# Half-array transposes beside the score matmuls, merged normalisation and tanh, in a fused attention and gated-convolution kernel

## The chip, the cores and the metric

The kernel runs on one core of one Trainium2 chip. The metric is the device time of one execution, in microseconds (us). A kernel was timed in three or more runs, beside runs of the kernel before on the same chip. "Fast" and "slow" are the states given to each run; with one core, slow means over 1.5% above the fastest run of the same kernel. The profile calls the engines PE (TensorE), DVE (VectorE), ACT (ScalarE), POOL (GpSimd) and SP (SyncE).

## The reference

q, k and v have shape (8, 8, 576, 64): 8 batches, 8 heads, 576 positions, 64 features.

```python
scores = scale * np.matmul(q, k.transpose(0, 1, 3, 2))
scores = np.where(block_i >= block_j, scores, -1e9)     # causal by blocks of 64
attn = softmax(scores);  x = attn @ v                   # heads side by side: (8, 576, 512)
gate_pre = sum(conv_w[k] * xp[:, k:k + S, :] for k in range(5))   # causal, per channel
return (sigmoid(gate_pre) * (x @ w_val)) @ w_out
```

## The kernel before

The work is cut into 32 pairs of heads, four to a batch. Each turn of the main loop computes the scores and exponentials of pair p, the weighted sum and normalisation of pair p-1, the query/key transposes of pair p+1, and a share of the convolution, of the value projection ("val") and of the output projection ("out") of an older batch. A "conv pair" (every second one) has a convolution. I call the loop up to pair 31 the loop, and what follows the start of pair 31 the drain. The last 64 positions of each batch, the "tails", are loaded, cast and transposed once per batch.

Every transpose uses the whole array: 8 for queries and keys, 5 for the attention output, 4 per batch for the tails. PE writes its results into four single-bank tiles G0 to G3 and two double-bank score tiles S.

```python
GT = [psG.tile([128, 512], fp32, tag=f"G{i}", name=f"G{i}") for i in range(4)]

def trans(p, bank=None):                       # cut: the special case of pair 0
    for i in range(2):
        for c in range(4):
            o = 512 * i + 128 * c
            nc.tensor.transpose(out=rr[i][:, o:o + 128], in_=t[0:128, c, 2 * i:2 * i + 2, 0:64],
                                identity=ident16[0:128, 0:128])
    # one DVE copy of 128x1024
    nc.vector.tensor_copy(out=o[0:128].rearrange("p i (s n) -> p i s n", n=4), in_=src[0])

def avs(p, banks):                             # weighted sum, then normalisation, head by head
    for h in range(2):
        av(p, h, banks[h])
        norm(p, h, banks[h])

# main loop, from pair 5 on (cut)
        s_tile(p, 0)
        s_tile(p, 1)
        avs(p - 1, (0, 1) if cv else (1, 0))
        if p < NP - 1:
            trans(p + 1, 2)
        if not early:
            out(3)
        ...
        s_tile(p, 2)
        mask(p)
        ...
        if cv:
            conv(gs // 2, (0, 1), early)
        xtrans(p - 1, 2 if cv else 0)
        # val, val
        if p in T_TRANS:                       # LAST thing in the turn
            trans_tails(T_TRANS[p], 2 if cv else 0 if early else 1)

# drain (cut): one output tile and one val alternate, over a ring of four banks
    for h in range(NP - LAG - 1, NP):
        for x in (0, 1):
            if len(outs) > 1:
                out()
            val(h // 2, 2 * (h % 2) + x)
```

Two tables decide where the tails of a batch are cast by POOL and where PE transposes them. From the fourth batch on, both are pair 4b-4: the same turn of the loop.

The softmax here doesn't subtract the row's maximum and nothing guards it: scores larger than these inputs give would overflow.

## Time and profile before

Median 199.47 us of the first three runs (198.42 to 202.71). The profiled run has a span of 196.9 us. I split it at the starts of the first score matmuls of pairs 0, 5, 13 and 31.

| stage | us | what limits it |
|---|---|---|
| head: pairs 0 to 4 | 19.65 | loads and first casts, then PE with holes |
| pairs 5 to 12 | 44.72 | PE, with holes |
| pairs 13 to 30 | 93.29 | PE, no holes: busy 93.30 of 93.30 us |
| drain | 32.08 | PE almost alone, no scores left |

From the page of the kernel before come three lines (those between are left out). They give each engine's busy time, the TensorE clock granted in 40 slices (tenths), and one group of instructions (busy time, mean ns of one, idle before it).

```profile
PE 181.9 (92%) x3701; PEld 124.3 (63%) x3701; DVE 131.8 (67%) x287; ACT 139.2 (71%) x193; POOL 81.1 (41%) x166
PEclk9999997999999999999999999999999999999999
L167 DVE COPY qkT<-G 128x1024 f16<-128x1024 f16 x31 | 37.7, 1217 | 3.7 <-PE G L156 3.5
```

The PE timeline of pair 19 before, a conv pair (start, duration, engine, line, operation, output<-input, count). A group's cost is read from start to start.

```profile
102.61 0.74 PE L33 MATMUL S<-qkT 64*128 64x512 f16 x6
103.28 0.60 PE L33 MATMUL G<-v,pt 128*128 128x65 f16 x14
...
104.20 0.61 PE L156 MATMUL G<-ident,qk 128*128 128x128 f16 x8
104.65 1.03 PE L33 MATMUL G<-w_out,gv 128*128 128x512 f16 x4
...
106.92 0.45 PE L252 MATMUL G<-ident,x 128*128 128x128 f16 x5
107.20 1.14 PE L33 MATMUL G<-xt,w_val 128*128 128x288 f16 x8
108.28 0.61 PE L33 MATMUL S<-qkT 64*128 64x512 f16 x6
```

Eight query/key transposes take 104.65 - 104.20 = 0.45 us and five output transposes 0.28: 56 ns each, 0.73 us together. The output projection follows the transposes without a gap.

### The profile page before, as it was taken

What the parts mean: (1) busy time and instruction counts of PE and PEld (TensorE: products, weight loads), DVE (VectorE), ACT (ScalarE), POOL (GpSimd) and SP (SyncE); (2) the same over time, 40 slices, a digit from 0 to 9 for tenths busy, and PEclk for the clock granted to TensorE, in tenths of its full rate; (3) what the DMA queues carried; (4) which work ended last, traced back from release to release, by engine and by line L of the source; (5) the groups of instructions that cost most, each with busy time, mean ns of one, the idle gap of its engine ahead of it and who ended that gap; (6) DMA issues with size and microseconds to landing.
All of it is one profiled execution on the core that took longest, in us unless ns stands there. A gap on an engine that the chain in (4) does not pass through costs nothing.

```text
span 196.9 us, 8701 instructions
## 1 busy us (share of the span) xinstructions
PE 181.9 (92%) x3701; PEld 124.3 (63%) x3701; DVE 131.8 (67%) x287; ACT 139.2 (71%) x193; POOL 81.1 (41%) x166
## 2 busy tenths in 40 slices
PE   3997859989799799999999999999999999999992
PEld 0475737666666477667667777677767675756550
DVE  5377756998668486768776767678676868542451
ACT  0778784777788788877888778887888797545321
POOL 7276742573564644345434543464445422100000
PEclk9999997999999999999999999999999999999999
DMA  5999999999999557976887687878665111143355
GB/s 159 258 285 258 264 326 314 218 261 220 268 226 289 154 170 195 271 223 178 228 249 224 190 243 215 235 215 238 203 201 145 57 57 57 58 158 149 133 208 213
DMA packets 70337, 40.43 MB, mean 205 GB/s; under 512 B 48149, under 2 KB 64789, under 8 KB 70298
## 3 DMA queue, kind: packets, MB, share of 16 engines
q1 hardware_dynamic: 68288, 39.07, 72.0%
q10 hardware_dynamic: 2010, 0.80, 1.8%
q8 instruction: 29, 0.48, 1.0%
q14 instruction: 10, 0.08, 0.2%
HBM read 30.42 MB, written 9.44 MB: 202 GB/s over the span
## 4 chain that ended last, share of the span: by engine, by line
PE 76%; DMA 9%; DVE 5%; SPq 3%; issue 2%; ACT 1%; ACTq 1%; POOL 1%; POOLq 0%; DVEq 0%
PE G L33 47%; PE S L33 17%; PE G L156 6%; PE G L252 5%; DMA tlst<-in_k_dram 3%; DMA qks<-in_k_dram 3%; DMA vs<-in_v_dram 3%; DVE w_val L388 2%; SPq L107 1%; DVE qkT L167 1%; DVE x L238 1%; SPq L86 1%; PE G L142 1%; DVE gv L292 1%; ACT pt L190 1%
## 5 line engine op out<-in xcount | busy, mean ns | idle before, releaser
L190 ACT ACTIVATE pt<-S 128x1024 f16<-128x1024 f32 x96 | 94.7, 1025 | 21.9 <-PE S L33 19.5
L206 POOL MEMSET pt<- 64x384 f16 x32 | 13.2, 412 | 76.5 <-ACT pt L190 76.3
L167 DVE COPY qkT<-G 128x1024 f16<-128x1024 f16 x31 | 37.7, 1217 | 3.7 <-PE G L156 3.5
L33 PE MATMUL G<-xt,w_val 128*128 128x288 f16 x256 | 38.7, 286 | 1.3 <-issue 1.3
L292 DVE SCALAR_TENSOR_TENSOR gv<-th,G 128x288 f16<-128x288 f32 x64 | 28.3, 453 | 14.0 <-PE G L33 12.3
L33 PEld LDWEIGHTS <-pt 128*128 128x128 f16 x960 | 32.1, 99 | 7.5 <-issue 3.5
L130 POOL CAST qk<-qks 128x1024 f16<-128x1024 f32 x31 | 32.4, 1047 | 10.1 <-DMA qks<-in_k_dram 8.1
L33 PE MATMUL G<-w_out,gv 128*128 128x512 f16 x144 | 36.5, 379 | 0.0
L33 PE MATMUL G<-v,pt 128*128 128x65 f16 x896 | 34.7, 195 | 1.6 <-POOL pt L206 1.1
L314 ACT COPY osb<-G 128x512 f32<-128x512 f32 x31 | 18.2, 587 | 22.2 <-PE G L33 19.5
L238 DVE TENSOR_TENSOR x<-G,rc 128x320 f16<-128x320 f32 x64 | 31.5, 492 | 2.2
L33 PE MATMUL S<-qkT 64*128 64x512 f16 (+1 forms) x248 | 29.1, 302 | 3.6 <-ACT pt L190 2.2
L33 PEld LDWEIGHTS <-qkT 64*128 64x128 f16 x496 | 16.1, 95 | 24.3 <-issue 20.0
L33 PEld LDWEIGHTS <-w_val 128*128 128x128 f16 x256 | 23.9, 98 | 8.9 <-issue 1.5
L237 DVE RECIPROCAL rc<-G 128x5 f32<-128x5 f32 x64 | 12.1, 189 | 20.1 <-PE G L33 20.0
L254 DVE COPY xt<-G 128x576 f16<-128x576 f16 x32 | 14.6, 456 | 13.3 <-PE G L252 13.0
L156 PE MATMUL G<-ident,qk 128*128 128x128 f16 x256 | 20.5, 225 | 2.2 <-DVE qk L127 1.8
L135 POOL CAST v<-vs 128x512 f16<-128x512 f32 x32 | 20.2, 632 | 0.5
L33 PEld LDWEIGHTS <-gv 128*128 128x128 f16 x144 | 12.9, 98 | 9.9
L156 PEld LDWEIGHTS <-qk 128*128 128x128 f16 x256 | 15.4, 101 | 4.2 <-DVE qk L127 2.7
L33 PE MATMUL G<-xt,DG 32*32 32x288 f16 x640 | 16.9, 288 | 0.3 <-DVE x L238 0.3
L33 PE MATMUL S<-xt,DG 32*32 32x288 f16 x640 | 16.8, 287 | 0.0
(58 smaller groups left out, 148.5 us busy)
## 6 DMA issues: line engine op xcount, KB each, us to landing
out_dram<-osb SPq DMA_DIRECT2D x35, 256.0 KB, 2.3
qks<-in_q_dram SPq DMA_DIRECT2D x32, 256.0 KB, 4.3
qks<-in_k_dram SPq DMA_DIRECT2D x31, 256.0 KB, 4.6
vs<-in_v_dram SPq DMA_DIRECT2D x62, 128.0 KB, 4.8
tlst<-in_q_dram SPq DMA_DIRECT2D x8, 128.0 KB, 4.6
vtst<-in_v_dram SPq DMA_DIRECT2D x8, 128.0 KB, 4.5
w_st<-in_moe_w_val_dram SPq DMA_DIRECT2D x2, 512.0 KB, 6.7
w_st<-in_moe_w_out_dram SPq DMA_DIRECT2D x2, 512.0 KB, 6.9
```

Source lines behind the costliest of these rows:

```text
L33: nc.tensor.matmul(out=out, lhsT=lhsT, rhs=rhs, start=start, stop=stop, skip_group_check=True)
L130: nc.gpsimd.tensor_copy(out=o, in_=s)
L135: nc.gpsimd.tensor_copy(out=v16s[p % NV][0:128, 0:4, 0:2, 0:64], in_=s)
L156: nc.tensor.transpose(out=rr[i][:, o:o + 128], in_=t[0:128, c, 2 * i:2 * i + 2, 0:64], identity=ident16[0:128, 0:128])
L167: nc.vector.tensor_copy(out=o[0:128].rearrange("p i (s n) -> p i s n", n=4), in_=src[0])
L190: nc.scalar.activation(out=pts[p % NPT][0:128, 0:2, 512 * t:512 * t + 512], in_=s[0:128, 0:2, 0:512], func=AF.Exp, bias=0.0, scale=0.125)
L206: nc.gpsimd.memset(pt[64:128, 0:2, 0:1536].rearrange("p h (t s) -> p h t s", t=3)[:, :, :, 0:64], 0.0)
L237: nc.vector.reciprocal(out=rc[0:128], in_=O[:, :, 64:65])
L238: nc.vector.tensor_tensor(out=x16[p][0:128, 0:5, h, 0:64], in0=O[:, :, 0:64], in1=rc[0:128].to_broadcast([128, 5, 64]), op=ALU.mult)
L254: nc.vector.tensor_copy(out=xts[b % NX][0:128, g, 4:4 + SEQ], in_=r[:, 0:SEQ])
L292: nc.vector.scalar_tensor_tensor(out=gv[u][0:128, x, bi, hf, 0:288], in0=t[0:128, x, 0:288], scalar=1.0, in1=r[0:128, 0:288], op0=ALU.add, ...
L314: nc.scalar.copy(out=o[0:128], in_=r[0:128, 0:512])
```

## The change

The intent is to halve the PE time of the transposes. Each is split in two 64-row halves that work in different row halves of the array and write to different banks, two at once. They move next to the score matmuls, which use the array in 64-row halves too. G0 and G1 become one two-bank tile G, so that one normalisation and one tanh cover both heads or both groups of channels. G2 and G3 (called GS) take all transposes.

```diff
-    GT = [psG.tile([128, 512], fp32, tag=f"G{i}", name=f"G{i}") for i in range(4)]
+    G = psG.tile([128, 2, 512], fp32, tag="G", name="G")
+    GS = [psG.tile([128, 512], fp32, tag=f"G{i}", name=f"G{i}") for i in (2, 3)]
+    def transpose(o, x, r):
+        hs = slice(64 * r, 64 * r + 64)
+        nc.tensor.transpose(out=o, in_=x, identity=ident16[hs, hs])
+    def trans_mm(p):                     # 16 half transposes; xt_mm: 9
+                for r in range(2):
+                    o = 256 * i + 64 * c
+                    transpose(half(r)[:, o:o + 64], t[64 * r:64 * r + 64, c, 2 * i:2 * i + 2, 0:64], r)
+    def norm(p):                         # both heads in one instruction
+        nc.vector.tensor_tensor(out=x[0:128].rearrange("p i h d -> p h i d"), in0=O[:, :, :, 0:64],
+            in1=rc[0:128].to_broadcast([128, 2, 5, 64]), op=ALU.mult)
     # main loop (cut)
         s_tile(p, 0)
         s_tile(p, 1)
-        avs(p - 1, (0, 1) if cv else (1, 0))
-        trans(p + 1, 2)
+        half_mm(p)              # q/k of p+1, output of p-2, and the TAILS if their pair has come
+        trans_ev(p + 1, 0)      # DVE copies, one per bank
+        xt_ev(p - 2, 0)
+        avs(p - 1)
+        norm(p - 1)
+        if cv:
+            out(2)
+            score()             # third score tile, mask
+            conv(gs // 2)
+            vals(h, (2, 3))
+        else:
+            score(); out(2)     # cut: `out` first in the pairs of T_LAST
+            vals(h, (0, 1))
-        if p in T_TRANS:
-            trans_tails(T_TRANS[p], ...)
     # drain (cut): two vals on the two banks of G, output tiles on G2 and G3
+        for i in range(2):
+            if len(outs) > 1:
+                out(2 + i)
+            if i == 0:
+                vals(h, (0, 1))
```

In the new order, pair 4b-4 transposes the tails in two rounds over two pairs.

## The prediction

> **What bounds it now.** The page gives TensorE (PE) 92% of the span and 76% of the chain that ended last. From 67 us to the end each 10 us window shows PE 9.9 to 10.0 busy, while VectorE (DVE) has about 7.3, ScalarE (ACT) 8, DMA 0.77. The timeline there repeats every 10.4 us per two head pairs (5.2 per pair) with practically no PE wait (PE on ACT: 2.2 us in the whole run). Between 27 and 67 us the PE does have holes (1.1 us for a POOL memset, 1.0 for ACT, about 2 for DVE behind the weight scaling); before 27 us the waits are DMA. The last 30 us (no scores left) are PE-dense again.
>
> **What the change removes.** In the timeline 8 query/key transposes take 0.45 us start to start, 5 output transposes 0.28: 56 ns each. Score matmuls 64x64 in the same kernel run as row-half pairs: 8 in 0.11 us, 28 ns a pair. If the half transposes pair likewise (16 and 9 instructions = 8 + 5 slots), they cost 0.22 + 0.14 us: 0.37 us less PE per pair, plus 0.11 per batch of tails. Switches: [...] the trace shows about 0.1 us more at each change (scores to full-array). But the old order has 9 changes per two pairs and so has the new: transposes only change sides. I count no gain there.
>
> **What it adds and moves, on DVE.** A 1024-element copy of 1217 ns becomes two of 512 (691 as measured for the first pair): +165 ns. The xt copy (456) becomes about 323 + 290: +157. Tails 420 become four of about 220. Normalisation (2 x (189+492)) becomes about 195 + 825: -340. Every second gate pair is merged: -150 per two pairs. Sum: about zero; DVE stays at 3.6 to 4 us a pair. Two tanh of 422 become one of 672: ACT little changed (about 4.1 us a pair start to start). Neither becomes the bound at 4.8 us a pair.
>
> **Critical path.** All PE savings are on it from 67 to 166 us (19 pairs, ideal 7 us). But fewer, shared banks give new waits: the merged normalisation is ready only after both halves, one copy chain frees the two transpose banks. Laying the durations end to end I find about 0.2 us of PE wait before the output projection in a conv pair, 0.2 where the half transposes wait for the previous gate, 0.5 per batch when tails copies go first. So I expect about 4.9 to 5.05 us a pair: 3 to 5 us saved. In 27 to 67 us: fewer bank conflicts with ACT, but the transposes now stand before the weighted sum and wait for the POOL cast: net -1 to -3 us. Tail: same work, two output banks instead of four, merged gates: +0 to +1.
>
> **Prediction.** 193.8 us, range 189.5 to 197.5. Faster by over 2%: 0.68; within 2%: 0.28; slower: 0.04.
>
> **What would show it.** Half transposes starting in pairs every 28 ns (right), or 16 taking 0.45 us again (wrong). Two-pair period of 9.7 to 10.1 us. PE waits on DVE (qkT/xt copies, normalisation, gate) appearing, some tenths of a us per pair; PE busy below 10 of 10. DVE busy total within 5 us of 132; ACT within 2 us of 139. Span before the first output projection shorter by 1 to 3 us.
>
> **What would make it wrong.** Half transposes that do not overlap (gain gone, about 199); DVE chain longer than laid out, so that conv and vals wait every pair (197+); or the new order hiding those waits fully and removing the holes before 67 us (189).

## More of the kernel before

The windows of the kernel before, one per stage. Columns are given in the header: window and its length, busy time and count of each engine, granted clock, DMA share and GB/s.

```profile
core 0: us, PE busy (x) PEld busy (x) DVE busy (x) ACT busy (x) POOL busy (x), PEclk, DMA share, GB/s
7.18:26.83 19.65, 16.17 (x295) 11.70 (x295) 13.61 (x29) 15.24 (x17) 12.24 (x21) 1.00 1.20 269
26.83:71.55 44.72, 39.86 (x901) 28.47 (x901) 32.63 (x70) 33.84 (x46) 22.18 (x39) 0.96 0.93 239
71.55:164.85 93.30, 93.30 (x2045) 65.58 (x2044) 68.20 (x148) 74.48 (x104) 41.47 (x79) 1.00 0.69 196
164.85:196.90 32.05, 28.39 (x451) 16.98 (x450) 13.18 (x31) 13.71 (x25) 1.64 (x5) 0.99 0.40 147
```

PE has no gap in the third stage and the full clock in it. DVE (68 of 93 us) and ACT (74 of 93) have slack.

## The result, and the profile after

A ratio below is the mean time of one kernel's fast runs over that of the other's in the same rounds, so it is not quite the ratio of the medians quoted with it. The kernel after took 218.05 us (median of four, 215.96 to 220.18), the kernel before beside it 198.94: ratio 1.095, 95% interval 1.082 to 1.108. It is slower by nearly a tenth. The output is correct.

The profiled run, at 220.18 us, is slow. Its mean granted clock (0.960) is like that of the three fast runs (0.958 to 0.967). I read waits and their places from it; the 2 to 4 us by which its span exceeds theirs are not placed. The three fast runs average 217.35 us. The profiles of e3, e8 and e14 are of runs labelled slow too.

| stage | before | after | difference |
|---|---|---|---|
| pairs 0 to 4 | 19.65 | 28.02 | +8.4 |
| pairs 5 to 12 | 44.72 | 45.15 | +0.4 |
| pairs 13 to 30 | 93.29 | 100.24 | +6.9 |
| drain | 32.08 | 37.97 | +5.9 |

The page of the kernel after, the lines that answer to those above (those between are left out). Its chain of work that ended last breaks off after 4% of the span, so stages and waits must serve instead.

```profile
PE 188.5 (86%) x4117; PEld 123.8 (57%) x4117; DVE 127.0 (58%) x295; ACT 138.8 (64%) x175; POOL 81.0 (37%) x166
PEclk9999959985999999999999799999999999999999
L165 DVE COPY qkT<-G 128x512 f16<-128x512 f16 x63 | 42.6, 683 | 15.1 <-PE G L140 15.1
```

The windows of the kernel after, the same stages and columns:

```profile
6.99:35.00 28.01, 23.07 (x354) 16.35 (x354) 14.46 (x35) 15.24 (x17) 13.20 (x22) 0.88 1.17 280
35.00:80.15 45.15, 37.75 (x996) 26.36 (x996) 30.83 (x76) 32.34 (x38) 21.47 (x40) 0.92 0.81 198
80.15:180.39 100.24, 92.95 (x2282) 62.23 (x2276) 64.73 (x149) 75.02 (x95) 41.63 (x79) 0.98 0.62 172
180.39:218.40 38.01, 30.78 (x472) 17.67 (x471) 12.98 (x24) 14.21 (x23) 1.05 (x3) 0.99 0.36 133
```

In the third stage PE is busy 92.95 of 100.24 us. It had no idle time there before and has 7.3 us now, about as much as the stage has grown. No other engine has become the limit: DVE and ACT are busy as long as before, in a longer stage. The PE waits for something, now and then.

The PE timeline of pair 19 after (the conv pair shown before):

```profile
113.08 0.89 PE L33 MATMUL S<-qkT 64*128 64x512 f16 x6
113.79 0.41 PE L140 MATMUL G<-ident,qk 64*128 64x64 f16 x16
114.02 0.31 PE L140 MATMUL G<-ident,x 64*128 64x64 f16 x9
114.26 0.60 PE L33 MATMUL G<-v,pt 128*128 128x65 f16 x14
...
115.15 0.20 PE L33 MATMUL G<-v16t,pt 128*128 128x65 f16 x1
115.41 1.02 PE L33 MATMUL G<-w_out,gv 128*128 128x512 f16 x4
...
117.67 1.15 PE L33 MATMUL G<-xt,w_val 128*128 128x288 f16 x8
118.76 0.61 PE L33 MATMUL S<-qkT 64*128 64x512 f16 x6
```

The half transposes pair as hoped: 16 in 0.23 us, or 28 ns for two. But the pair takes 5.68 us against 5.67. The output projection starts 0.26 us after the last weighted-sum matmul, where one slot is 0.03: it waits for its bank.

PE, then POOL, in pair 20 after, the first pair of a batch's tails. In brackets: idle before, and the releaser.

```profile
119.20 0.56 PE L140 MATMUL G<-ident,qk 64*128 64x64 f16 x16
119.59 0.31 PE L140 MATMUL G<-ident,x 64*128 64x64 f16 x9
121.48 0.23 PE L140 MATMUL G<-ident,tl 64*128 64x64 f16 x4 [1.59 <-POOL tl L116]
121.65 0.60 PE L33 MATMUL G<-v,pt 128*128 128x65 f16 x14
```

```profile
118.72 1.04 POOL L130 CAST qk<-qks 128x1024 f16<-128x1024 f32 x1
119.69 0.62 POOL L135 CAST v<-vs 128x512 f16<-128x512 f32 x1
120.25 0.62 POOL L119 CAST v16t<-vtst 128x512 f16<-128x512 f32 x1
120.81 0.62 POOL L116 CAST tl<-tlst 128x512 f16<-128x512 f32 x1
```

The tails' cast is the fourth in POOL's queue of this very pair and ends at 121.43; PE stands still for 1.59 us until then. In the kernel before the same cast had the whole pair to finish in. The list of PE's waits after has as its first line:

```profile
PE G L140 <- POOL tl L116: 6.6, 5, 1.6
```

That is 6.6 us in five waits. Something more follows. Pair 20 takes 7.75 us, against 4.77 for an ordinary pair without convolution, and the wait accounts for only 1.6 of the 3.0. The granted clock is at half from 122.4 to 125.8 us. It is also at half from 26.8 to 33.6 and 47.3 to 54.1 us, and, by the durations of its matmuls (under "The clock" below), before 23.4 us.

### The profile page after: what moved, and what is told of

It reads as the page before. It is cut to its first block, busy times and chain, and to the rows that moved or that the text cites. A ratio compares the mean times of both kernels' runs of the same rounds, so it can differ in the third digit from the quotient of the medians.

```text
span 218.4 us, 9500 instructions
## 1 busy us (share of the span) xinstructions
PE 188.5 (86%) x4117; PEld 123.8 (57%) x4117; DVE 127.0 (58%) x295; ACT 138.8 (64%) x175; POOL 81.0 (37%) x166
## 5 line engine op out<-in xcount | busy, mean ns | idle before, releaser
L203 ACT ACTIVATE pt<-S 128x1024 f16<-128x1024 f32 x96 | 94.6, 1024 | 32.4 <-PE S L33 30.2
L165 DVE COPY qkT<-G 128x512 f16<-128x512 f16 x63 | 42.6, 683 | 15.1 <-PE G L140 15.1
L293 DVE SCALAR_TENSOR_TENSOR gv<-th,G 128x288 f16<-128x288 f32 (+1 forms) x49 | 26.0, 544 | 35.7 <-PE G L33 34.1
L33 PE MATMUL G<-v,pt 128*128 128x65 f16 x896 | 37.5, 202 | 0.5 <-ACT w_out L401 0.3
L33 PE MATMUL S<-qkT 64*128 64x384 f16 (+3 forms) x256 | 33.1, 324 | 4.2 <-ACT pt L203 2.7
L33 PEld LDWEIGHTS <-pt 128*128 128x128 f16 x960 | 34.8, 103 | 2.2
L250 DVE TENSOR_TENSOR x<-G,rc 128x640 f16<-128x640 f32 x32 | 26.4, 824 | 1.1
L140 PE MATMUL G<-ident,qk 64*128 64x64 f16 x512 | 16.0, 197 | 3.8 <-POOL qk L130 2.0
L178 DVE COPY xt<-G 128x320 f16<-128x320 f16 x64 | 17.1, 297 | 1.6 <-PE G L140 1.6
L140 PEld LDWEIGHTS <-qk 64*128 64x128 f16 x512 | 12.1, 100 | 9.1 <-POOL qk L130 2.9
L33 PEld LDWEIGHTS <-DG 32*32 32x32 f16 x1280 | 12.7, 88 | 7.9 <-issue 5.6
```

The costliest lines, as they stand in the source:

```text
L33: nc.tensor.matmul(out=out, lhsT=lhsT, rhs=rhs, start=start, stop=stop, skip_group_check=True)
L140: nc.tensor.transpose(out=o, in_=x, identity=ident16[hs, hs])
L165: (cp or nc.vector.tensor_copy)(out=qkT[p][0:128, 0:2, 256 * r:256 * r + 256].rearrange("p i (s n) -> p i s n", n=4), in_=half(r)[:, 0:512 ...
L178: nc.vector.tensor_copy(out=xts[b % NX][0:128, g, 4:644].rearrange("p (i r s) -> p i r s", r=2, s=64)[:, 0:n, r], in_=half(r)[:, 512:512 + ...
L203: nc.scalar.activation(out=pts[p % NPT][0:128, 0:2, 512 * t:512 * t + 512], in_=s[0:128, 0:2, 0:512], func=AF.Exp, bias=0.0, scale=0.125)
L250: nc.vector.tensor_tensor(out=x[0:128].rearrange("p i h d -> p h i d"), in0=O[:, :, :, 0:64], in1=rc[0:128].to_broadcast([128, 2, 5, 64]), ...
```

## The experiments

**The theories.** (A) The halves do what they should; the new order lost more than they save, by waits that PE did not have before, and these waits also cost clock. (B) The halves themselves harm: half-array work is too slow, or makes PE lose the full clock. (C) The merged instructions harm, by making PE wait for the later half. Fourteen kernels ran, all with correct results (no label e6 was used); the befores of the jobs were 198.3 to 199.97 us. Medians are compared with the kernel after (218.05) or with the kernel that was edited; where slow runs shift a median, the mean of the fast runs is given beside it.

### e1_cast: cast the tails one pair earlier

```diff
-    T_LOAD = {{1: 0, 2: 4, 3: 7}.get(b, 4 * b - 6): b for b in range(1, B)}
-    T_CAST = {{1: 3, 2: 7, 3: 9}.get(b, 4 * b - 4): b for b in range(1, B)}
+    T_LOAD = {{1: 0, 2: 4, 3: 7}.get(b, 4 * b - 7): b for b in range(1, B)}
+    T_CAST = {{1: 3, 2: 6, 3: 9}.get(b, 4 * b - 5): b for b in range(1, B)}
```

> The tail tiles (last 64 rows of q and k of a batch) are loaded and cast one head pair earlier, nothing else. Theory A (the POOL cast that the half transposes now wait for at the start of a pair costs 1.3 to 1.8 us of PE at pairs 16, 20, 24 and about 1.1 at pair 7, and the long idle also drops the TensorE clock at 47 and 122 us): the PE wait on POOL tl disappears, pairs 16, 20, 24 last 4.9 to 5.1 us instead of 6.0 to 7.8, the half-clock stretch at 122 us goes, and the kernel is 5 to 8 us faster than the changed one (210 to 213). Rival (half transposes are slow or the new chain of copies holds every pair): the wait moves to another engine and the time stays within 2 us of 218.

Measured: 209.15 us, ratio 1.054 (1.044 to 1.064). Pair 20 in e1:

```profile
114.03 0.31 PE L140 MATMUL G<-ident,x 64*128 64x64 f16 x9
114.16 0.24 PE L140 MATMUL G<-ident,tl 64*128 64x64 f16 x4
```

The hole is gone, and the three tails pairs 16, 20 and 24 take 4.53 us each instead of 6.29, 7.75 and 6.03. An edit of two tables is worth 8.9 us (7.9 by the fast runs alone: 209.43 against 217.35), more than its waits: with them went the half-clock stretches near 122 us and from 47 to 54 us. So the order of the queue on POOL was one of the two largest losses, beside the head. The stage of pairs 13 to 30 is still 95.07 us against 93.29 before, so the saving on the transposes is not yet seen.

### e2_warm: eight warm-up matmuls instead of four

The kernel issues dummy matmuls at its start. Their number is doubled.

```diff
-    warm(4)
+    warm(8)
     cast_qk(0, first=True)
```

> Eight dummy matmuls instead of four before the first transposes, so that the PE has no 2 us hole while the first loads arrive. Theory A (the head lost 8 us because the clock reached full speed at 23 to 34 us instead of 8 us[...]): full clock from about 5 to 8 us, pair 5 starts near 28 us instead of 35, total 5 to 8 us less (210 to 213). Rival ([...] the head order itself is slow): pair 5 still starts after 33 us and the total stays within 2 us of 218.

Measured: pairs 0 to 4 in 21.61 us, not 28.02, as expected. The total, 217.24 us (214.32 to 221.96; the two fast runs average 215.36), did not follow: 210 to 213 was expected. The clock row of e2's page:

```profile
PEclk9999699959999999969999799969999999999998
```

The kernel now reaches the full clock in the head, but loses it again near the tails' waits, at 93.3, 117.2 and 141.1 us. In the kernel after only one of these waits, at 122.4 us, did so in pairs 13 to 30. The head and the tails' waits are tied by the clock: with the tails' waits still there (7.1 us in six, 6.6 in five in the kernel after), a mend of the head raised the falls behind them in pairs 13 to 30 from one to three.

### e3_drain: output tiles and vals over four banks again, as before

In the drain, single vals and a ring of four banks, while the two-bank tile G stays.

```diff
+        ring = (0, 1, 2, 3) if h % 2 and h < NP - 1 else (2, 3, 0, 1)
+        for x in (0, 1):
+            if len(outs) > 1:
+                out(ring[2 * x])
+            val1(h // 2, 2 * (h % 2) + x, ring[2 * x + 1])
```

> The old drain in the changed kernel: after the last scores, values are gated one at a time and outputs and values go round all four banks. Theory A (two output banks and the merged gate and tanh make the PE wait 5 to 6 us in the drain): from the start of pair 31 to the end 33 to 34 us instead of 38, total 4 to 5 us less (213 to 214). Rival (the drain is longer for another reason, for example one more output tile and slower copies): under 1.5 us less.

A miss: the drain grew from 37.97 to 41.14 us, the total was 222.05 (fast runs: 220.3). The drain of e3 shows why:

```profile
189.13 1.02 PE L33 MATMUL G<-w_out,gv 128*128 128x512 f16 x4
190.87 0.65 PE L33 MATMUL G<-xt,w_val 128*128 128x288 f16 x4 [0.72 <-ACT osb L328]
```

The val writes one bank of G, and waits for ACT's copy of an output tile out of the other bank of G. A two-bank tile is one unit of dependence here; whether the chip or the framework makes it one is not shown. My edit had mixed two things, four banks and a tile that is only one unit; it says nothing against four independent banks.

### e4_all: e1, e2 and e3 together

The edit is the three diffs above, with no other line changed.

> The three edits together. If the three losses are separate and are all of the slowdown: about 199 to 202 us, the same as the kernel before within 2%, with regular pairs still at 10.4 to 10.5 us for two, so the saved PE time is still lost in them. If the losses overlap or something else is in play: above 205. If the regular pairs get faster once the stalls are gone: below 197.

A miss: 211.09 us, not 199 to 202. The drain took 41.14 us again (e3's fault), and pairs 0 to 4 took 25.65: the same head as e2's got the full clock at 4.3 us and lost it from 7.8 to 18.0. Pairs 13 to 30 took 93.00 us with every four pairs in 20.73, so even without holes the pairs only equal the before's 20.82. The 0.37 us per pair were still hidden by something in the ordinary pairs.

### e5_score_first: third score tile ahead of the output projection (on e1)

```diff
         if cv:
+            score()
             if not early:
                 out(2)
-            score()
             conv(gs // 2)
         ...
+            score()
+            out(2)
             vals(h, (0, 1))
```

> As e1_cast, and the last score tile of a pair is issued before the output projection in all late pairs, so the projection meets its bank after the transposes' copies are done. Theory A (in regular pairs the saved 0.37 us is given back by the projection waiting 0.16 to 0.23 us for the copies out of the transposes' bank, and by the exp that then comes late for the next pair's scores): conv pairs 5.4 us instead of 5.68, pairs with the last scores 4.6 instead of 4.77, about 0.7 us per four pairs, 2 to 4 us in all against e1_cast (205 to 207). Rival (ScalarE or VectorE holds the period, whatever the order on the PE): pairs keep 5.68 and 4.77, time within 1 us of e1_cast.

Measured: 203.76 us (ratio 1.023, 1.013 to 1.034, so unclear whether over 2% slower than before) against 209.15 for e1; 205 to 207 was expected, so a little better than that. Part of the 5.4 us is another phase of the clock in the head (24.56 against 27.34), and part is two single holes in e1's pairs 23 and 27 (0.8 and 1.7 us) that e5 does not have. In the loop, four pairs take 20.10 instead of 20.72. Start to start, PE spends in the conv pair 19:

| us | before | after | e5 |
|---|---|---|---|
| two score tiles | 0.67 | 0.71 | 0.44 |
| query/key and output transposes | 0.73 | 0.47 | 0.47 |
| weighted sums, to the next group | 0.92 | 1.15 | 1.03 |
| third score tile, output projection, convolution | 2.27 | 2.26 | 2.28 |
| two vals | 1.08 | 1.09 | 1.08 |
| sum | 5.67 | 5.68 | 5.30 |

(The numbers of before and after can be checked on the two timelines above; the before's 0.73 is 0.45 + 0.28. A "mode" below is the division of the array: matmuls on 64 rows or on all 128.) The transposes save 0.26 in the kernel after. They are paid back by 0.23 at the end of the weighted sums, where the output projection waits for its bank until DVE has copied the transposes out of it, and by 0.04 at the score tiles. The latter should have become 0.1 shorter, as in pair 18 (0.54 us before, 0.44 after), since no change of mode follows them any more; instead they wait 0.27 us against e5. In both kernels ACT copies the output tile before it does the exponential of the third score tile (in pair 18 the copy starts at 100.90 and the exponential at 101.38 us before, 111.52 and 112.00 after), and so frees the score tiles late. The same place in e5, where the score tile now stands before the output projection:

```profile
106.07 0.20 PE L33 MATMUL G<-v16t,pt 128*128 128x65 f16 x1
106.20 0.28 PE L33 MATMUL S<-qkT 64*128 64x256 f16 x2
106.53 1.04 PE L33 MATMUL G<-w_out,gv 128*128 128x512 f16 x4
```

With the scores first, the third score tile fills the time of DVE's copies and its exponential comes before the output copy: 0.12 and 0.27 us come back. In the pair without convolution the sum is 4.69 before, 4.77 after and 4.66 in e5. There the half transposes still wait 0.15 us for the previous gate on G3.

So these two pairs take 9.96 us (10.05 is the mean over four pairs): the "two-pair period of 9.7 to 10.1 us" that was predicted exists, but only in this order.

### e7_unmerged: four separate banks, single normalisation, tanh and gates (on e1)

```diff
-    G = psG.tile([128, 2, 512], fp32, tag="G", name="G")
-    GS = [...]
+    GT = [psG.tile([128, 512], fp32, tag=f"G{i}", name=f"G{i}") for i in range(4)]
+    GS = GT[2:4]
     # norm per head, tanh in three parts, single gates, and e3's drain
```

> As e1_cast, with the merging undone: four separate bank tiles, normalisation per head, tanh in three parts, single gates, and the old drain going round the four banks. Only the half transposes and their place are left of the change. Theory A (the merged two-bank tile is one unit for dependencies, so in the drain conv, tanh, values and outputs wait for each other; run e3 mixed a ring of four with that one unit and so got worse): from pair 31 to the end 32 to 33.5 us instead of 38, regular pairs within 0.2 us of e1_cast, total 203 to 206. Rival (the drain is long because of something that the half transposes or the one more output tile do): drain stays at 36 to 38 and the total at 208 or more.

Measured: 206.75 us (ratio 1.037, 1.026 to 1.049), just above the 203 to 206 that I expected. The drain took 34.00 us with the same code that took 41.14 in e3, which confirms the reading of e3. Pairs 14 to 17 and 18 to 21 took 21.28 and 20.89 us, 0.2 to 0.6 more than e1's 20.71 and 20.73 (pair 15 of e7 and later pairs of both hold single holes). Merging therefore costs the loop nothing and may help it by 0.2 us per four pairs; in the drain it goes with 3.9 us (37.87 to 34.00). Theory C holds for the drain only.

### e8_full_array: full-array transposes in the new order (on e1)

```diff
-    transpose(half(r)[:, o:o + 64], t[64 * r:64 * r + 64, c, 2 * i:2 * i + 2, 0:64], r)
+    transpose(half(0)[:, o:o + 128], t[0:128, c, 2 * i:2 * i + 2, 0:64])
     # query/key into G2 with one copy of 1024, output and tails into G3 with one copy
```

> As e1_cast, with full-array transposes in the new place and the new banks, merging kept. If the half arrays are worth their 0.37 us per pair: four regular pairs take 1 to 1.5 us more than in e1_cast (20.7), total 4 to 7 us more (213 to 216). If the waits set the period: four pairs within 0.4 us of 20.7, total within 2.5 us of e1_cast. Part of a rise comes from the one copy of 1024 elements that then frees the projection's bank 0.3 us later; that shows as a longer wait before the projection in conv pairs.

Measured: 221.29 us, of which two runs of four were slow; the two fast runs average 219.0, about 10 us worse than e1's 209.4 and above the 213 to 216 expected. The head was cold until 24.6 us with full-array transposes too (23.4 in the kernel after). Theory B falls on the first count: the halves are not too slow. On the clock it is not settled. A cold head does not need halves, but after 24.6 us e8 kept the full clock to its last matmuls, where e1 lost it at 26.1 us; a count under "The clock" below speaks for B.

### e9_drain_S: vals of the drain on the free score banks (on e1)

```diff
-                vals(h, (0, 1))
+        vals(h, (0, 1), S())         # S(): a score tile, free in the drain
```

> As e1_cast, but in the drain the values use the score banks, which are free by then, and the last outputs go round three tiles. All else merged as in the changed kernel. Theory A (conv, tanh, gates and values share the one merged tile, and two output banks are too few): 33 to 34.5 us from pair 31 to the end instead of 38, total 4 to 5 us below e1_cast (204 to 206). Rival (DVE and ACT copies are what is slow in the drain): less than 1.5 us gained.

Measured: drain 34.24 us (37.87 in e1), total 206.83 us against the 204 to 206 expected. The drain of the kernel after, then of e9:

```profile
196.06 1.04 PE L33 MATMUL G<-w_out,gv 128*128 128x512 f16 x4
197.38 1.14 PE L33 MATMUL G<-xt,w_val 128*128 128x288 f16 x8 [0.29 <-ACT th L281]
```

```profile
184.53 1.04 PE L33 MATMUL G<-w_out,gv 128*128 128x512 f16 x4
185.40 1.14 PE L33 MATMUL S<-xt,w_val 128*128 128x288 f16 x8
```

In the first, the vals after a convolution start 1.32 us after the output tile, since G still holds the convolution that ACT has to read for tanh. In e9 they start 0.87 us after it, without a wait. The merged instruction stays, but not only its bank is another: e9's edit (cut above) also starts each convolution before the output tile and lets some output tiles use the score banks. So the loss in the drain is one of banks and order, not of merging as such; bank and order were not parted.

### e10_head and e11_three: the mends together

e11 is e1 + e5 + e9. e10 is e11 with a new head: eight warm-up matmuls, the first tails' transposes four at once in place of two rounds, the tails of pairs 3 and 4 after the mask, and two dummy matmuls on G3 in place of G's bank 0, where they had waited for the normalisation.

```diff
-    warm(4)
+    warm(8)
-            for gs in ((0, 1), (2, 3)):
-                tails_mm(0, gs)
-                tails_ev(0, gs)
+            tails_mm(0, (0, 1, 2, 3), 512)
+            tails_ev(0, (0, 1, 2, 3), 512)
+        late_tails(p)              # pairs 1 to 4, after mask(p); in half_mm only from pair 5 on
-            warm(2, 0)
+            warm(2, 3)
```

> The same three mends (e1, e5, e9) without the new head. If the losses add: e5 (203.8) less the 3.7 us of e9's drain, 199 to 202 us; the difference to e10 is then the head alone, 3 to 7 us. If they do not add: above 203.

> All mends together: tail cast one pair early (e1), scores before the output projection (e5), the drain on the score banks (e9), and the head of the old kind: the tails' transposes of the first batches all at once or after the pair's last score tile instead of waiting at its start, dummy matmuls that do not wait for the normalisation, eight dummies at the start. Theory (the four losses are separate and the half arrays are worth 0.6 to 0.8 us per four pairs): first five pairs 20 to 22 us, pairs 13 to 31 90 us, drain 34.3, total 194 to 198, at or below the kernel before. Rival (the head's clock is lost whatever the fillers[...]): first five pairs 25 us or more, total 199 to 203.

Measured: e11 201.62 us (ratio 1.013), a hit. e10 201.1 us (1.016), a miss: 194 to 198 was expected. The head came close to the before's (20.30 us against 19.65) and pairs 13 to 30 took 90.11 us, 3.2 less than the before's. But pairs 5 to 12 took 47.10. My own earlier cast of the second batch's tails, in pair 6, stood waiting in POOL's queue for 4.15 us and held PE up for 2.9. Before that, the clock was at half from 24.8 to 38.5 us.

### e12_head_only: that head on the kernel after, alone

The edit is the diff just shown, on the kernel after.

> The changed kernel with the new head alone. Theory: first five pairs 20 to 23 us instead of 28; the rest as in the changed kernel (its tail waits can drop the clock one to three times, 3 us each), total 209 to 214. Rival (half transposes keep the clock low): first five pairs stay above 25 us, total 216 or more.

Measured: pairs 0 to 4 in 20.24 us, as expected, and 215.07 us in all, a little above the expected 209 to 214. Of the 7.8 us gained in the head only 3.0 are left (2.0 by the fast runs alone). The half clock came back at 13.3, 40.6, 115.7 and 139.6 us. This is e2's lesson again: the head cannot be mended alone while the tails' waits stay. Which of the new head's edits mends it was not parted; the eight warm-up matmuls alone gave 21.61 us in e2.

### e13_before_warm: the kernel before with eight warm-up matmuls

The same edit as e2's (`warm(4)` to `warm(8)`), on the kernel before.

> Control: the kernel before with eight dummy matmuls at the start instead of four, as in e10. It tells whether the filler would help the old kernel as well: it reaches full clock at about 8 us already, so at most 1.5 us faster (197 to 199); if it gained 3 us or more, e10 would have to be compared with this kernel.

Measured: 196.89 us, ratio 0.995 (0.991 to 0.998). It is the fastest kernel, by half a per cent. In its profile the clock is full from 6.9 us to the last matmuls, where the profile of the kernel before loses it once (28.8 to 32.2 us).

### e14_batch2: e10 with the second batch's tails at the end of pair 7

```diff
-    T_CAST = {{1: 3, 2: 6, 3: 9}.get(b, 4 * b - 5): b for b in range(1, B)}
+    T_CAST = {{1: 3, 2: 7, 3: 9}.get(b, 4 * b - 5): b for b in range(1, B)}
+        if p == 7:
+            tails_mm(2, (0, 1, 2, 3), 512)
+            tails_ev(2, (0, 1, 2, 3), 512)
```

> As e10_head, but the tails of batch 2 are cast in pair 7 as before (in pair 6 the cast kept the POOL queue waiting 4 us and the PE 3.5 us) and transposed at the end of pair 7. Theory (that hole, and the half clock from 25 to 38 us that went with the holes in this stretch, is what kept e10 above the kernel before): pairs 5 to 13 take 42 to 44 us instead of 47, total 195 to 198, that is 1 to 2% below the kernel before. Rival (the half arrays leave the clock marginal in the loading phase wherever the waits are): pairs 5 to 13 stay above 45 us, total 199 or more.

Measured: 199.63 us (196.47 to 200.66) beside 198.9 before, ratio 0.998 (0.989 to 1.007). With all losses found so far mended, the change equals the kernel before. The median misses the 195 to 198 expected, but three of the six runs were slow: the fast ones average 197.85, inside it. Pairs 5 to 12, at 44.62 us in the profile of a slow run, miss the 42 to 44. The clock was at half from 20.9 to 24.3 and from 31.1 to 34.6 us. Across the three fast runs the time falls with the mean granted clock: 199.40 us at 0.980, 197.68 at 0.983, 196.47 at 0.991.

### e15_full_mended: e14 with full-array transposes

The edit is e8's, on e14.

> As e14_batch2, with full-array transposes in place of the half ones (same place, same banks, one copy of 1024 and one of 576). It weighs the half arrays where the waits have been taken out. Theory (half arrays are worth the 0.37 us of PE per pair there): four regular pairs 21.3 to 21.9 us instead of 20.1, pairs 13 to 31 5 to 7 us longer, total 4 to 8 us above e14. Rival (half arrays are worth nothing or harm): four regular pairs within 0.4 us of 20.1, total within 2 us of e14 or below it.

Measured: 211.55 us, on the same chip as e14's 199.63. Four pairs take 22.79 us instead of 20.11, or 0.67 per pair. By the fast runs, 211.6 against 197.85, the halves with their copies are in this order worth about 14 us, more than the 4 to 8 expected and more than the 0.37 of bare PE time per pair. Part of the rest shows in pairs 13 to 30 as waits of PE for DVE, which now makes one long copy in place of two: 1.9 us for the query/key copy and 1.5 for the normalisation, against 0.3 in e14. So e15 weighs the halves together with their copies. The halves suit this order; they do not show that the order as a whole beats the old one. The halves in the old order were not run.

## Why the prediction was wrong, point by point

Predicted 193.8 us (189.5 to 197.5), measured 218.05. Both the direction and the size were wrong.

- **The halves pair: right.** 16 in 0.23 us, as estimated (0.22). That this saves PE time in the loop is shown, together with their copies, by e14 against e15. Pairs 13 to 30 in e14 take 90.12 us, 3.2 less than before with the same 18 output tiles, inside the predicted "3 to 5 us saved"; but it took e1's and e5's edits to get there.
- **Changes of mode neutral: right.** In the trace the two score tiles of pair 18 take 0.54 us before a full-array group (kernel before) and 0.44 to 0.45 before the half transposes (kernel after, e5): 0.1 us per change. The change moved from there to the end of the transposes: nine halves take 0.24 us to the first weighted-sum matmul in pair 19 after, where five slots of 28 ns are 0.14.
- **DVE and ACT not the bound: right.** DVE busy 131.8 to 127.0 us and ACT 139.2 to 138.8, within the margins named. Halving the elements did not halve a copy: 1217 ns for 1024 before, 683 for 512 after, so two of 512 cost 149 ns more than one of 1024.
- **The failed step** is "But fewer, shared banks give new waits ... 0.2 us ... 0.2 ... 0.5 per batch when tails copies go first. So I expect about 4.9 to 5.05 us a pair". It looked only at banks and at DVE. In place of 3 to 5 us saved, pairs 13 to 30 took 6.9 us more: 5.57 us a pair on average, against 5.18 before.
  - The waits of 0.2 for the output projection and 0.2 for the gate were there, 0.23 and 0.15 us.
  - The 0.5 per batch was a wait for POOL of 1.3 to 1.6 us, with the clock lost behind one of the three in pairs 13 to 30, because a transpose moved from the end to the start of the pair that casts its input. The tables had not changed, so the diff did not show it. I named a wait for a POOL cast, but only for the query/key casts before 67 us. e1 recovers 8 to 9 us.
  - ACT's order, the output copy ahead of the exponential, was not looked at. With the bank wait it returned the transposes' saving in every conv pair; e5's order recovers 0.62 us per four pairs.
- **"27 to 67 us: net -1 to -3 us": wrong.** Pairs 5 to 12 grew by 0.4 us although one output tile of 0.95 us had left them, and pairs 0 to 4 by 8.4. I did not think of the clock: PE first got it in full at 23.4 us instead of 8.3. Holes alone are not the reason, since from 9.7 to 16.6 us PE was busy 6.77 of 6.83 us and stayed at half. A new head (e12), which also removes some waits, takes it back to 20.24 us.
- **"Tail ... +0 to +1": wrong by 5 us.** The drain grew by 5.9. The term was named, "two output banks instead of four, merged gates", but not costed. Vals on other banks (e9) or separate tiles (e7) recover 3.6 to 3.9; of the remaining 2 us about 0.9 is one more output tile left for the drain (18 where the kernel before has 17), and the rest is open.
- **The wrong-case list** named halves that do not overlap and a longer DVE chain. Neither happened; "slower" got a chance of 0.04 because I listed no engine but PE and DVE as the source of waits.

**The clock, as far as it is shown.** The half-clock stretches between two full ones are all multiples of 3.41 us: 3.41 in the kernel before (from 28.77 us), 6.83, 6.83 and 3.41 in the kernel after (from 26.79, 47.27 and 122.36 us). So are the full ones between them (13.65 and 68.27 us in the kernel after). I therefore look at PE's work in windows of 3.41 us that end where the clock could change. Long holes are not needed: in the three windows before the falls in the kernel after the longest hole was 1.16, 0.95 and 1.59 us. Nor does PE's busy time in a window decide. Four windows in the kernel after, then one in e12:

```profile
13.14:16.55 3.41, 3.41 (x46) 2.86 (x47) 1.92 (x4) 1.76 (x2) 2.50 (x5) 1.00 1.18 290
95.06:98.47 3.41, 2.35 (x57) 1.41 (x39) 0.87 (x2) 3.23 (x5) 2.79 (x6) 1.00 0.90 276
118.95:122.36 3.41, 1.82 (x58) 1.43 (x55) 0.98 (x4) 2.05 (x3) 2.48 (x4) 1.00 0.82 234
142.84:146.25 3.41, 2.09 (x59) 1.49 (x58) 1.24 (x5) 2.27 (x3) 2.53 (x4) 1.00 0.82 234
```

```profile
9.87:13.28 3.41, 2.73 (x52) 2.01 (x51) 2.23 (x5) 2.02 (x3) 2.83 (x6) 1.00 1.17 295
```

(The clock column shows 1.00 in the first line because the trace has no clock record before 23.38 us. That it was half shows in the durations: 14 weighted-sum matmuls at 15.53 us took 0.95 us, the same at 114.26 us 0.60.) In the first PE is busy all the time, and the clock stays at half; in the kernel before it came back after a window with PE busy 2.95 us (28.77 to 32.18 us). The next three hold the tails' waits of pairs 16, 20 and 24: the clock falls after pair 20's alone. In e12 it falls after a window with PE busy 2.73 us.

A count from the matmul records of all 16 traces fits much better. Add up the input columns of the matmuls that start in a window, each matmul's weighted with the share of the 128 rows that it uses. The five windows above count about 2770, 4130, 3000, 3380 and 2570. Before all 30 drops inside the kernels the count was at most 3072. Of the 505 windows without convolution that kept the full clock, one had 2954 and all others 3072 or more. In the two kernels alone, falls came after counts of 2176 (before), 1635, 1568 and 3000 (after), and the full clock was kept after 3382 or more. (Windows with convolution are left out, because I do not know how its 32-row tiles would count. A few matmul records can be missing.) Going back to full speed took 3072 or more as well, but counts up to 3146, and 3583 in one case, were also seen to stay at half. So half-array work seems to count by half. This is an estimate worked out from the traces and not tested by a run of its own; nor was it tested whether transposes count. If it holds, the halves help to lose the clock: the 29 half transposes in pair 20's window count 928, as full-array ones they would count 1856, and the window 3930 instead of 3000. It also fits that e2 and e12, whose windows lie elsewhere against the waits, lost the clock more often: behind all three tails' waits of pairs 16, 20 and 24 in e2 (93.3, 117.2, 141.1 us), and at 13.3, 40.6, 115.7 and 139.6 us in e12.

**Other things left open.** Single PE holes of 0.6 to 2.1 us without any semaphore wait appear once or twice in several profiles (kernel before at 64.6 us, kernel after at 164.0, e3 at 141.5), with no cause found. Each of these three follows within 2 us the start of a transfer on the DMA queue that the page calls "instruction" (63.1, 162.2 and 141.3 us), but such transfers also come every 4 to 8 us without a hole, so this is a hint only. e14 loses in the first 13 pairs (2.1 us: 66.47 against 64.37) and in the drain (2.3) what it gains in pairs 13 to 30. Whether the halves in this order with a clean clock and a better drain would beat e13 was not tried.

## What to carry to other kernels

When work moves to another place in a loop, look up for each of its inputs where in its producer's queue that input is made. A table that the diff leaves alone can turn a harmless distance into a wait of over a microsecond per turn. Count the result banks and the order on the copying engine again in every stage (head, loop, drain), since a PE saving per pair returns as a wait wherever the old order had been filling the time. Keep PE dense over every few microseconds: here a hole of 1.59 us made its pair 3.0 us longer when the clock fell behind it, half-array work may count by half towards keeping the clock (the estimate above), and a mend of one stage can move the loss to another (of the 7.8 us that e12 gained in the head 3.0 were left).
